# DeltaNet with mixture-of-depths: the query-key products masked on other engines, one join product moved to another PSUM bank, and a re-tuned plan

## The chip, the cores and the metric

The kernel runs on one core of a Trainium2 chip. A core has a matrix engine (TensorE, "PE" in the profile, with its weight loads as "PEld"), VectorE (DVE), ScalarE (ACT), GpSimd (POOL) and SyncE (SP), which issues most DMAs. Each engine works through its own queue in order and waits at semaphores for the others. The metric is the device time of one execution, in microseconds (us).

## The reference

Inputs are q, k, v of shape (batch 4, heads 8, 768 tokens, head size 48) and beta. For each of the 32 batch-head pairs a 48x48 state is carried over the tokens; its output is then the input x of a mixture-of-depths block.

```python
k_n = k / (norm(k) + 1e-6)
for t in range(768):
    y[t] = q[t] @ state                              # read before the update
    state += beta[t] * outer(k_n[t], v[t] - k_n[t] @ state)

x = y as (4, 768, 384)
scores = x @ w_gate
for b in range(4):
    top = the 128 tokens of the highest score
    out = x;  out[top] += sigmoid(scores[top]) * (relu(x[top] @ w1) @ w2)
```

## The kernel before

The tokens are cut into chunks of 64. Batches go in two groups of two, so there are 24 units (`NU`): chunks 0 to 11 of group 0, then chunks 0 to 11 of group 1. Within a chunk the recurrence is a triangular system. Its 64x64 matrices are cut into 32x32 diagonal blocks, and those of four units (128 of them, one on each partition) are inverted together: that is an *elimination* (`eliminate(e)`, six of them, e = 0 to 5).

- `prep(i)`: transposes k and q through PSUM (L437), copies them out on ACT (L442), multiplies k by k (to `gs`, spilled to DRAM by SP, L503, and read back as `a`) and q by k (to `p`). The q-k product lies in two PSUM banks of the ring `inv` (three banks). In the kernel before, DVE takes it out and masks it with the strict upper triangle in one instruction for each bank (`out_p`, L507): 48 in all.
- `eliminate(e)`: all on DVE but two steps. The norms (L567 to L582), the scaling of `a` (L592), a copy of `a` into PSUM by ACT (`lift`, L596), the unit diagonal (L599), 30 pairs of a multiply (L608) and a subtract (L615), each of which needs the one before, the mask (`final`, L621) and two transposes (`turn_out` L624, `turn_back` L628). POOL makes the table `mb` (L585) and copies half-blocks of `tt` (`lows`, L716).
- `join(e, m)`: for each unit of the four, PE makes `z` (L688, L690), ACT copies it (`ez`, L694), PE makes two products (L701, L703), ACT copies them into `tt` (`ej`, L710).
- `recur(i)`: the chain from unit to unit: PE `mm_r` into `prec` (L750), DVE adds it to v (L757), PE `mm_w` (L763), two ACT copies (L768), PE `mm_s` (L774), two ACT copies (L781), and then the next unit's `mm_r`. Beside it `mm_q` (L790) and `mm_p` (L801) build the output in the bank `py`, and ACT takes it out (L807). `mm_p` needs the masked `p`. POOL scales v (L742) and multiplies the output by the gate weights (L824).
- `ranking(g)` and `depths(b)`: comparisons of the scores (POOL L909 and L913, at the very end DVE), their sums on PE (L937), the choice (DVE L979), gather, two layers (L1035, L1049), scatter. Those of group 0 are mixed in with the recurrence of group 1; those of group 1 are the tail.

The order on every engine is written by `Plan`: a list scheduler that runs when the program is built. Each step has a length, dependences, a priority (`prio`; smaller goes first) and tokens that it takes and gives back (`ring`, such as the three `inv` banks). Whatever the planner's times are, what runs on the chip is the resulting order on each queue. Where it foresees a gap on PE, it puts in filler matmuls (`filler`, L348) that have no use but to keep PE active.

Of the kernel before, what the change touches and what calls it, by code (L numbers as in the profile page):

```python
# [185 lines left out]
def kernel(  # L186
# [24 lines left out]
    GP = GB * HP  # L211
    GI = GP // 2
# [18 lines left out]
    plan = Plan()  # L231
    rings = {}
# [36 lines left out]
    py = psum.tile([P, 512], FP32, name="py")  # L269
# [5 lines left out]
    rings["late"] = [ap[:, m] for m in range(2)]  # L275
    plan.ring("late", 2)
    first_g = rings["tt"][1]

    def got(*key):
        name, m = plan.live[key]  # L280
        return rings[name][m]

    def maker(eng, own=0.0, lat=0.15):
        def add(dur, emit, deps=(), prio=0.0, take=(), give=(), lat=lat, hard=False, ins=0,
                dmas=0, moves=0.56, room=None):
            op = plan.add(eng, dur, emit, deps, prio,
                          [(t[0] if isinstance(t, tuple) else t, t) for t in take],
                          give, lat)
            op.own, op.hard, op.ins, op.dmas = own, hard, ins, dmas
            op.moves, op.room = moves, room  # L290
            return op
        return add

    pe, act, dve, pool, sp = [maker(*e) for e in (
        ("PE", 0.0, 0.22), ("ACT", 0.0, 0.12), ("DVE", 0.12, 0.2), ("POOL",), ("SP",))]
# [135 lines left out]
    N = {}  # L431
# [14 lines left out]
    def prep(i):  # L446
# [10 lines left out]
        def bank(key):  # L457
            return got(*key)[:, :GI * C].rearrange("p (r t) -> p r t", t=C)
# [46 lines left out]
        def out_p(rt):  # L505
            def emit():
                nc.vector.tensor_tensor(  # L507
                    out=got("p", i).rearrange("p (r b) t -> p r b t", b=2)[:, :, rt],
                    in0=bank(kw[rt]), op=ALU.mult,
                    in1=up[:, None, :].to_broadcast([P, GI, C]))  # L510
            return emit

        n["lk"] = sp(0.65 if first else 1.25,
# [6 lines left out]
        for nm in "kq":  # L520
            emit, put = turn(i, nm)
            v, h = (u - 2, hard) if nm == "k" else (10 * i - 20, {})
            n["t" + nm] = pe(0.46, emit, [n["l" + nm]], v, ins=2 * GI,
                             take=[("inv", i, nm), (nm + "t", i)],
                             give=[("q", i)] if nm == "q" else [], **h)
            n["e" + nm] = act(0.6, put, [n["t" + nm]], v, give=[("inv", i, nm)], **h)
# [4 lines left out]
        else:  # L531
# [8 lines left out]
                    ins=16 * GI, lat=0.8)  # L540
        n["ep"] = [dve(0.43, out_p(rt), [n["w"]], v, give=[kw[rt]]) for rt in range(2)]

    def eliminate(e):
# [98 lines left out]
        N["nrm", e] = s["nt"] = dve(0.2, turn_n, [s["sc"]], u + 2)  # L642
        s["mb"] = pool(1.3, table, [s["sc"]], u, take=[("mb", e)])
        last = dve(1.2, scale, [s["sc"]], u, **hard)
# [8 lines left out]
        N["steps", e] = last  # L653
        last = dve(1.15, final, [last, s["mb"]], u, **hard)
        N["final", e] = last
# [13 lines left out]
    def join(e, m):  # L669
# [5 lines left out]
        s, n = N["e", e], N[i]  # L675
        key = {w: ("inv", i, w) for w in ("z", "ja", "jb")}

        def view(w):
            return got(*key[w])[:, :GI * HC].rearrange("p (n t) -> p n t", t=HC)

# [47 lines left out]
    def recur(i):  # L728
# [98 lines left out]
        def total():  # L827
# [4 lines left out]
                     take=[("v", i)], dmas=2, room=1.0)  # L832
        x = r["vh"] = pool(1.1, vh, [n["lv"], N["e", e]["nt"]], u - 12, lat=0.3)
        if c > 0:
# [15 lines left out]
        if c > 0:  # L850
            r["q"] = pe(0.7, mm_q, qdep + [*o["es"], n["eq"], o.get("xo")], u + 3, ins=8 * GI)
            pdep = [r["q"]]
        r["p"] = pe(0.7, mm_p, [*r["w"], *n["ep"], o.get("xo")] + qdep + pdep, u + 3, ins=8 * GI,
                    give=[("kt", i), ("qt", i), ("p", i)])
        plan.add("PE", 0.0, lambda: None, [r["p"], r.get("s")], 10 * i, give=[("k", i)])
        r["xo"] = act(0.48, out_x, [r["p"]], u + 4, take=[("x", j)] if i % 2 == 0 else [],
                      lat=0.12 if i == NU - 1 else 2.0)
        late = i >= NU - 2
        if late:
            N["score", i] = dve(0.65, score, [r["xo"], N["wg"]], u + 12, give=[("x", j)])  # L860
        else:
            pr0 = pool(1.1, score, [r["xo"], N["wg"]], u + 12, take=[("prod", i)],
                       give=[("x", j)], lat=1.0)
            N["score", i] = act(0.52, total, [pr0], u + 14, give=[("prod", i)])
# [9 lines left out]
    def ranking(g):  # L874
# [4 lines left out]
        def stage(j0, j1, prev):  # L879
# [75 lines left out]
            for j in range(j0, j1):  # L955
                d.append((dve if soon else pool)(
                             0.37 + 0.26 * (j > 0) + 0.067 * j if soon else
                             0.5 + 0.08 * (j + 1), above(j), [a1] + (d or tests)[-1:], u + 1,
                             take=[km] if j == j0 else [],
                             give=[("rep", g)] if last else [], **hd))  # L960
# [178 lines left out]
```

## Time and profile before

| | |
|---|---|
| median of three runs | 331.19 us (330.13 to 333.48) |
| the profiled execution | 330.42 us |
| its span in the trace | 328.6 us |
| PE busy | 294.1 us, of it 51.3 us fillers |
| DVE busy | 210.3 us |
| ACT busy | 177.1 us |
| POOL busy | 126.5 us |

Busy times of a stretch are sums over an engine's instructions. Matmuls are pipelined, so a PE that shows 90% is not at its peak. A wait counts only if the engine that waits is the one that others wait for in that stretch. The first 57 us are loading and elimination 0, 57 to 283 us the recurrence of the 24 units, the rest the tail.

### The profile page before, as it was taken

What the parts mean: (1) busy time and instruction counts of PE and PEld (TensorE: products, weight loads), DVE (VectorE), ACT (ScalarE), POOL (GpSimd) and SP (SyncE); (2) the same over time, 40 slices, a digit from 0 to 9 for tenths busy, and PEclk for the clock granted to TensorE, in tenths of its full rate; (3) what the DMA queues carried; (4) which work ended last, traced back from release to release, by engine and by line L of the source; (5) the groups of instructions that cost most, each with busy time, mean ns of one, the idle gap of its engine ahead of it and who ended that gap; (6) DMA issues with size and microseconds to landing.
All of it is one profiled execution on the core that took longest, in us unless ns stands there. A gap on an engine that the chain in (4) does not pass through costs nothing.

```text
span 328.6 us, 15204 instructions
## 1 busy us (share of the span) xinstructions
PE 294.1 (90%) x6583; PEld 229.5 (70%) x6603; DVE 210.3 (64%) x580; ACT 177.1 (54%) x490; POOL 126.5 (39%) x199
## 2 busy tenths in 40 slices
PE   7879999899979999689959989799988999989993
PEld 2766444688857887468847867588877898667781
DVE  6037999798866889979878799759991102342000
ACT  1446000877667768677576864765876566211120
POOL 8105103721482338426293463820827243122011
PEclk9959999999997999999985999879999799999999
DMA  7967896246876486835764229526301021102000
GB/s 129 139 113 162 189 276 200 40 118 154 165 145 144 117 161 108 216 88 93 159 126 92 58 103 182 102 50 128 81 6 48 4 51 27 26 26 64 8 26 24
DMA packets 116083, 34.05 MB, mean 104 GB/s; under 512 B 108432, under 2 KB 112656, under 8 KB 116016
## 3 DMA queue, kind: packets, MB, share of 16 engines
q1 hardware_dynamic: 113392, 31.11, 45.0%
q0 software_dynamic: 512, 1.57, 1.5%
q8 instruction: 52, 0.85, 1.1%
q10 hardware_dynamic: 2112, 0.39, 0.8%
q14 instruction: 15, 0.12, 0.1%
HBM read 22.32 MB, written 10.75 MB: 101 GB/s over the span
## 4 chain that ended last, share of the span: by engine, by line
PE 66%; issue 10%; ACT 8%; DVE 6%; POOL 5%; DMA 2%; SPq 1%; POOLq 0%; ACTq 0%; DVEq 0%
PE inv L348 13%; PE prec L763 6%; PE inv L437 6%; PE inv L491 5%; PE psta L774 5%; PE py L801 4%; PE ap L1035 4%; PE py L790 4%; PE prec L750 4%; PE ap L1049 3%; POOL mk L909 3%; ACT wbd L768 2%; PE inv L701 2%; PE inv L1035 2%; PE inv L1049 2%
## 5 line engine op out<-in xcount | busy, mean ns | idle before, releaser
L615 DVE TENSOR_TENSOR ap<-ap,tmp 128x30 f32<-128x30 f32 (+9 forms) x180 | 60.5, 336 | 5.0
L608 DVE TENSOR_TENSOR tmp<-a,ap 128x30 f32<-128x30 f32 (+9 forms) x180 | 58.5, 325 | 5.0
L348 PE MATMUL inv<-warm 128*128 128x512 bf16 x187 | 51.3, 401 | 5.3 <-DVE warm L362 2.1
L824 POOL TENSOR_TENSOR prod<-x,wg 128x384 f32<-128x384 f32 x22 | 23.9, 1088 | 37.4 <-ACT x L807 37.2
L742 POOL TENSOR_TENSOR v<-v,nnT 128x384 f32<-128x384 f32 x24 | 19.7, 828 | 47.0 <-DMA v<-in_v_dram 46.9
L348 PEld LDWEIGHTS <-warm 128*128 128x128 bf16 x207 | 19.8, 102 | 23.0 <-issue 3.3
L909 POOL TENSOR_SCALAR mk<-rep 128x64 bf16<-128x64 f32 (+11 forms) x22 | 27.5, 1250 | 19.0 <-ACT rep L901 16.2
L768 ACT COPY wbd<-prec 64x384 f32<-64x384 f32 x48 | 22.7, 473 | 16.2 <-PE prec L763 11.6
L757 DVE TENSOR_TENSOR v<-v,prec 128x384 f32<-128x384 f32 x22 | 12.2, 553 | 28.7 <-PE prec L750 15.3
L716 POOL COPY tt<-tt 32x256 f32<-32x256 f32 x48 | 19.5, 406 | 25.4 <-DVE tt L624 21.1
L710 ACT COPY tt<-inv 32x128 f32<-32x128 f32 x96 | 24.6, 256 | 7.5 <-PE inv L703 5.4
L763 PEld LDWEIGHTS prec<-v,tt 64*64 64x64 f32 x768 | 25.2, 138 | 4.8 <-issue 2.4
L763 PE MATMUL prec<-v,tt 64*64 64x48 f32 x768 | 28.1, 223 | 0.3
L781 ACT COPY s<-psta 64x384 f32<-64x384 f32 x44 | 20.8, 473 | 9.9 <-PE psta L774 9.5
L774 PE MATMUL psta<-wbd,k 128*48 128x96 f32 x352 | 21.5, 268 | 3.8 <-ACT wbd L768 2.9
L774 PEld LDWEIGHTS psta<-wbd,k 128*48 128x48 f32 x352 | 16.5, 133 | 9.4 <-ACT wbd L768 6.2
L801 PE MATMUL py<-wbd,p 128*64 128x96 f32 x384 | 21.8, 260 | 0.0
L585 POOL TENSOR_SCALAR_AFFINE_SELECT mb<-bh 128x1024 f32<-128x1024 f32 x6 | 11.6, 1941 | 24.9 <-DVE bh L579 24.9
L442 ACT COPY kt<-inv 128x512 f32<-128x512 f32 x24 | 14.1, 591 | 13.1 <-PE inv L437 12.9
L790 PE MATMUL py<-s,qt 128*64 128x96 f32 x352 | 20.1, 260 | 0.0
L507 DVE TENSOR_TENSOR p<-inv,up 128x256 f32<-128x256 f32 x48 | 19.5, 415 | 0.4 <-PE inv L491 0.2
L801 PEld LDWEIGHTS py<-wbd,p 128*64 128x64 f32 x384 | 18.7, 147 | 1.2 <-ACT spr L890 0.5
(151 smaller groups left out, 609.4 us busy)
## 6 DMA issues: line engine op xcount, KB each, us to landing
gd<-gs SPq DMA_DIRECT2D x20, 256.0 KB, 2.9
v<-in_v_dram SPq DMA_DIRECT2D x48, 96.0 KB, 3.2
q<-in_q_dram SPq DMA_DIRECT2D x48, 96.0 KB, 3.1
k<-in_k_dram SPq DMA_DIRECT2D x44, 96.0 KB, 3.5
out_dram<-x SPq DMA_DIRECT2D x20, 192.0 KB, 3.2
a<-gd SPq DMA_DIRECT2D x20, 128.0 KB, 3.4
w_sb<-in_moe_w_dram SPq DMA_DIRECT2D x3, 512.0 KB, 4.9
w_sb<-in_moe_w_dram SPq DMA_DIRECT2D x4, 384.0 KB, 4.6
```

Source lines behind the costliest of these rows:

```text
L348: nc.tensor.matmul(rings[name][k], lhsT=warm[:, :P], rhs=warm, start=True, stop=True)
L608: nc.vector.tensor_tensor(out=view(), op=ALU.mult, in0=got("a", e)[:, j + 1:, j:j + 1].to_broadcast([P, w, j]), in1=blocks[:, j:j + 1, :j] ...
L615: nc.vector.tensor_tensor(out=a[:, j + 1:, :j], in0=a[:, j + 1:, :j], in1=view(), op=ALU.subtract)
L710: nc.scalar.copy(to[lo[par], :, int(w == "jb"), HC:], view(w)[lo[par]])
L763: nc.tensor.matmul(pw[half[par], a], lhsT=tt[half[par], ch * GP + a], rhs=x[half[par], a], start=True, stop=True)
L768: nc.scalar.copy(wb[half[par], :, par], pw[half[par]])
L774: nc.tensor.matmul(psta[ds[a % 2], a // 2], lhsT=t[:, a, :D], rhs=wb[:, a].rearrange("p h d -> p (h d)"), start=(c == 0 and a < 2), stop=True,
L781: nc.scalar.copy(s_new[half[rt], :, :, rt], psta[half[rt]].rearrange("p a (x d) -> p a x d", d=D))
L790: nc.tensor.matmul(pyv[half[bb], h4, :, par], lhsT=qt[:, bb * 2 + h4, half[par]], rhs=s_old[:, bb * 2 + h4, par], start=(h4 == 0 and par = ...
L801: nc.tensor.matmul(pyv[half[bb], h4, rt], lhsT=t[:, a], rhs=wb[:, a], start=(c == 0 and h4 == 0 and rt == 0), stop=True, skip_group_check= ...
L824: nc.gpsimd.tensor_tensor(out=got("prod", i), in0=got("x", i // 2)[:, i % 2], in1=wg, op=ALU.mult)
L909: nc.gpsimd.tensor_scalar(out=mk[:, :(j + 1) * C].rearrange("p (j c) -> p j c", c=C), in0=rep[:, :j + 1, :C], scalar1=rep[:, j, C:], scala ...
```

## The change

Four things. (1) The q-k product is copied out of PSUM by ACT, unmasked, and POOL then masks all of it in place in SBUF, with one instruction for each unit. (2) `z` is written to columns 384 to 511 of the bank `py`, which the output (columns 0 to 383) leaves free, and no longer to an `inv` bank; `py` becomes a ring of one, taken by `mm_q` (or `mm_p` where there is none) and given back by the copy L807, and taken by `z` and given back by `ez`. (3) Some lengths in the plan are set to other values. (4) A table `SHIFT` adds an offset to the priority of 50 kinds of steps.

```diff
+SHIFT = {
+    "ACT:<lambda>": -28.4, "ACT:ej": 7.8, "ACT:ez": -7.3, "ACT:gate0": -2.7, "ACT:lift": -12.0,
...
+    "turn_k": -26.5,
+}
+def kind(eng, emit):
...
+    rings["py"] = [py]
+    plan.ring("py", 1)
+    assert DM + GI * HC == 512
...
-            op = plan.add(eng, dur, emit, deps, prio,
+            op = plan.add(eng, dur, emit, deps, prio + SHIFT.get(kind(eng, emit), 0.0),
...
         def out_p(rt):
             def emit():
-                nc.vector.tensor_tensor(
-                    out=got("p", i).rearrange("p (r b) t -> p r b t", b=2)[:, :, rt],
-                    in0=bank(kw[rt]), op=ALU.mult,
-                    in1=up[:, None, :].to_broadcast([P, GI, C]))
+                nc.scalar.copy(got("p", i).rearrange("p (r b) t -> p r b t", b=2)[:, :, rt],
+                               bank(kw[rt]))
             return emit
+
+        def mask():
+            t = got("p", i)
+            nc.gpsimd.tensor_tensor(out=t, in0=t, op=ALU.mult,
+                                    in1=up[:, None, :].to_broadcast([P, GP, C]))
...
-            n["t" + nm] = pe(0.46, emit, [n["l" + nm]], v, ins=2 * GI,
+            n["t" + nm] = pe(0.9, emit, [n["l" + nm]], v, ins=2 * GI,
...
-        n["ep"] = [dve(0.43, out_p(rt), [n["w"]], v, give=[kw[rt]]) for rt in range(2)]
+        n["ep"] = [act(0.38, out_p(rt), [n["w"]], v, give=[kw[rt]]) for rt in range(2)]
+        n["ep"] = [pool(1.3, mask, n["ep"], v)]
...
-        s["mb"] = pool(1.3, table, [s["sc"]], u, take=[("mb", e)])
+        s["mb"] = pool(1.8, table, [s["sc"]], u, take=[("mb", e)])
...
-        key = {w: ("inv", i, w) for w in ("z", "ja", "jb")}
+        key = {w: ("inv", i, w) for w in ("ja", "jb")}
+        key["z"] = ("py", i, "z")
...
-            r["q"] = pe(0.7, mm_q, qdep + [*o["es"], n["eq"], o.get("xo")], u + 3, ins=8 * GI)
+            r["q"] = pe(0.7, mm_q, qdep + [*o["es"], n["eq"]], u + 3, ins=8 * GI, take=[("py", i)])
...
-                             0.5 + 0.08 * (j + 1), above(j), [a1] + (d or tests)[-1:], u + 1,
+                             0.6 + 0.16 * (j + 1), above(j), [a1] + (d or tests)[-1:], u + 1,
```

What the change does to the order is seen at three places. Line numbers of the changed kernel are about 30 higher: L638 and L645 are the multiply and subtract of the elimination, L789 the addition to v, L539 the mask on POOL.

The first is DVE in elimination 1, around the addition of unit 1 (`v1`), before:

```order
L615 TENSOR_TENSOR ap_141<-ap_141,tmp_170 128x23x8
L608 TENSOR_TENSOR tmp_170<-a1_112,ap_141 128x198
L757 TENSOR_TENSOR v1_79<-v1_79,prec_139 128x384
L615 TENSOR_TENSOR ap_141<-ap_141,tmp_170 128x22x9
L608 TENSOR_TENSOR tmp_170<-a1_112,ap_141 128x210
L507 TENSOR_TENSOR p1_102<-inv0_136,up_153 128x4x64
L615 TENSOR_TENSOR ap_141<-ap_141,tmp_170 128x21x10
L507 TENSOR_TENSOR p1_102<-inv2_138,up_153 128x4x64
L608 TENSOR_TENSOR tmp_170<-a1_112,ap_141 128x220
```

and of the change:

```order
L638 TENSOR_TENSOR tmp_170<-a1_112,ap_141 128x198
L645 TENSOR_TENSOR ap_141<-ap_141,tmp_170 128x22x9
L638 TENSOR_TENSOR tmp_170<-a1_112,ap_141 128x210
L645 TENSOR_TENSOR ap_141<-ap_141,tmp_170 128x21x10
L638 TENSOR_TENSOR tmp_170<-a1_112,ap_141 128x220
L645 TENSOR_TENSOR ap_141<-ap_141,tmp_170 128x20x11
L789 TENSOR_TENSOR v1_79<-v1_79,prec_139 128x384
L638 TENSOR_TENSOR tmp_170<-a1_112,ap_141 128x228
L645 TENSOR_TENSOR ap_141<-ap_141,tmp_170 128x19x12
```

The masking is gone from between the steps, and the addition stands five steps later.

The second is DVE where elimination 2 is prepared (`a0`): the scaling, the transpose of the norms, and the memset of the diagonal, which waits for ACT's `lift`. Before:

```order
L579 TENSOR_TENSOR bh0_168<-bh0_168,bt_143 128x32
L592 TENSOR_TENSOR a0_111<-a0_111,bh0_168 128x1024
L582 STREAM_TRANSPOSE nnT2_167<-nrm_164 128x32
L599 MEMSET ap_141 128x32
L608 TENSOR_TENSOR tmp_170<-a0_111,ap_141 128x30
L615 TENSOR_TENSOR ap_141<-ap_141,tmp_170 128x30
```

and of the change, whose memset L629 stands two rows behind the last one shown:

```order
L622 TENSOR_TENSOR a0_111<-a0_111,bh0_168 128x1024
L638 TENSOR_TENSOR tmp_170<-a1_112,ap_141 128x84
L789 TENSOR_TENSOR v3_81<-v3_81,prec_139 128x384
L645 TENSOR_TENSOR ap_141<-ap_141,tmp_170 128x3x28
L612 STREAM_TRANSPOSE nnT2_167<-nrm_164 128x32
L638 TENSOR_TENSOR tmp_170<-a1_112,ap_141 128x58
L645 TENSOR_TENSOR ap_141<-ap_141,tmp_170 128x2x29
L638 TENSOR_TENSOR tmp_170<-a1_112,ap_141 128x30
L645 TENSOR_TENSOR ap_141<-ap_141,tmp_170 128x30
L651 TENSOR_TENSOR a1_112<-ap_141,mb1_120 128x1024
L654 STREAM_TRANSPOSE tt1_124<-a1_112 128x32x32
L658 STREAM_TRANSPOSE mb1_120<-a1_112 128x32x32
```

The scaling of block 2 now stands ahead of the end of block 1, so that the two transposes lie between the mask of block 1, behind which `lift` may start, and the memset.

The third is POOL at the join of elimination 3: `lows` (L716, now L748) and the comparisons of the ranking (L909, now L941). Before:

```order
L585 AFFINE_SELECT mb_119<-bh_168 128x1024
L824 TENSOR_TENSOR prod_129<-x_126,wg 128x384
L909 TENSOR_SCALAR mk_130<-rep_127 128x576
L913 TENSOR_TENSOR mk_130<-mk_130,trib 128x64
L909 TENSOR_SCALAR mk_130<-rep_127 128x640
L913 TENSOR_TENSOR mk_130<-mk_130,trib 128x64
L716 COPY tt_124<-tt_124 32x8x32 x8
L824 TENSOR_TENSOR prod_129<-x_126,wg 128x384
```

and of the change:

```order
L941 TENSOR_SCALAR mk_130<-rep_127 128x512
L945 TENSOR_TENSOR mk_130<-mk_130,trib 128x64
L774 TENSOR_TENSOR v_81<-v_81,nnT_165 128x384
L856 TENSOR_TENSOR prod_129<-x_125,wg 128x384
L748 COPY tt_124<-tt_124 32x8x32 x4
L539 TENSOR_TENSOR p_104<-p_104,up 128x512
L748 COPY tt_124<-tt_124 32x8x32 x4
L615 AFFINE_SELECT mb_119<-bh_168 128x1024
L856 TENSOR_TENSOR prod_129<-x_126,wg 128x384
```

The two long comparisons are no longer ahead of `lows`, and a mask stands between its halves.

On PE the order has 107 fillers where it had 207; the q-k products of units 1 to 3, the k-k products of units 8 to 11 and the transposes that these need now stand ahead of the first `z`; the transposes of beta (L304) stand behind all products of the first four units, where they stood in the middle; and two `z` never stand next to each other. Ahead of the end of elimination 5, DVE now has the addition of unit 18 as its last, where it had that of unit 19.

## Rows read from the trace of the kernel before

**Rows 1.** The page's first part: busy us (share) x instructions of each engine.

```profile
PE 294.1 (90%) x6583; PEld 229.5 (70%) x6603; DVE 210.3 (64%) x580; ACT 177.1 (54%) x490; POOL 126.5 (39%) x199
```

**Rows 2.** Busy time by stretch: PE, PEld, DVE, ACT, POOL; granted clock; DMA.

```profile
57.00:247.00 190.00, 170.75 (x4725) 141.85 (x4738) 159.11 (x436) 134.38 (x377) 88.46 (x115) 0.95 0.55 115
247.00:283.00 36.00, 33.66 (x769) 28.67 (x767) 5.01 (x14) 23.18 (x70) 15.63 (x22) 0.95 0.13 32
```

**Rows 3.** Timeline of DVE, eliminations 0 and 1: start, length, line [idle before].

```profile
28.18 0.09 DVE L599 MEMSET ap<- 128x32 f32 x1 [1.06 <-ACT ap L596]
...
50.40 1.23 DVE L621 TENSOR_TENSOR a<-ap,mb 128x1024 f32<-128x1024 f32 x1
...
59.65 0.09 DVE L599 MEMSET ap<- 128x32 f32 x1 [1.01 <-ACT ap L596]
```

**Rows 4.** Timeline of DVE at the end of elimination 5.

```profile
241.56 1.23 DVE L621 TENSOR_TENSOR a<-ap,mb 128x1024 f32<-128x1024 f32 x1
```

**Rows 5.** Timeline of DVE: the same steps without masking (elimination 0) and with (1).

```profile
34.14 0.37 DVE L608 TENSOR_TENSOR tmp<-a,ap 128x210 f32<-128x210 f32 x1
34.55 0.39 DVE L615 TENSOR_TENSOR ap<-ap,tmp 128x210 f32<-128x210 f32 x1
...
66.66 0.38 DVE L608 TENSOR_TENSOR tmp<-a,ap 128x210 f32<-128x210 f32 x1
66.95 0.42 DVE L507 TENSOR_TENSOR p<-inv,up 128x256 f32<-128x256 f32 x1
67.28 0.38 DVE L615 TENSOR_TENSOR ap<-ap,tmp 128x210 f32<-128x210 f32 x1
```

**Rows 6.** The page's groups: the masking on DVE.

```profile
L507 DVE TENSOR_TENSOR p<-inv,up 128x256 f32<-128x256 f32 x48 | 19.5, 415 | 0.4 <-PE inv L491 0.2
```

**Rows 7.** Waits: who waited for whom, us in total, times, longest.

```profile
DVE v L757 <- PE prec L750: 15.3, 10, 4.8
...
DVE ap L599 <- ACT ap L596: 7.9, 5, 2.7
```

**Rows 8.** Timelines of PE and DVE at the start.

```profile
15.04 0.87 PE L304 MATMUL inv<-ident,both 32*64 32x16 f32 x24 [1.38 <-issue]
...
21.05 1.95 DVE L551 STREAM_TRANSPOSE a<-tt 128x1024 f32<-128x1024 f32 x1 [4.06 <-ACT tt L481]
```

**Rows 9.** Groups nearest to what is added: busy us, mean ns, idle before.

```profile
L824 POOL TENSOR_TENSOR prod<-x,wg 128x384 f32<-128x384 f32 x22 | 23.9, 1088 | 37.4 <-ACT x L807 37.2
...
L498 ACT COPY gs<-inv 128x256 f32<-128x256 f32 x40 | 13.1, 374 | 6.2 <-PE inv L491 6.1
...
L807 ACT COPY x<-py 128x384 f32<-128x384 f32 x24 | 11.5, 481 | 4.9 <-PE py L801 4.5
...
L694 ACT COPY zt<-inv 128x128 f32<-128x128 f32 x24 | 6.4, 267 | 15.4 <-PE inv L690 15.0
```

**Rows 10.** Timelines of DVE and POOL: the scaling and the table side by side.

```profile
127.41 1.23 DVE L592 TENSOR_TENSOR a<-a,bh 128x1024 f32<-128x1024 f32 x1
127.45 2.31 POOL L585 TENSOR_SCALAR_AFFINE_SELECT mb<-bh 128x1024 f32<-128x1024 f32 x1 [1.45 <-DVE bh L579]
...
161.97 1.27 POOL L585 TENSOR_SCALAR_AFFINE_SELECT mb<-bh 128x1024 f32<-128x1024 f32 x1 [6.41 <-DVE bh L579]
```

**Rows 11.** Timeline of DVE: the additions of units 19, 21 and 23.

```profile
238.89 0.55 DVE L757 TENSOR_TENSOR v<-v,prec 128x384 f32<-128x384 f32 x1 [0.19 <-PE prec L750]
...
260.61 0.55 DVE L757 TENSOR_TENSOR v<-v,prec 128x384 f32<-128x384 f32 x1 [4.77 <-PE prec L750]
...
273.41 0.56 DVE L757 TENSOR_TENSOR v<-v,prec 128x384 f32<-128x384 f32 x1 [5.64 <-ACT x L807]
```

**Rows 12.** The chain that ended last, in the tail: start, length, what.

```profile
301.40 5.39 PE inv L1035 x48
```

**Rows 13.** Timeline of POOL at the join of elimination 3.

```profile
164.19 1.72 POOL L909 TENSOR_SCALAR mk<-rep 128x576 bf16<-128x576 f32 x1
...
168.99 3.49 POOL L716 COPY tt<-tt 32x256 f32<-32x256 f32 x8
```

More of the change, by code (lines that the diff above doesn't have):

```diff
@@ L21 @@
 LAND = 2.6
+SHIFT = {
+    "ACT:<lambda>": -28.4, "ACT:ej": 7.8, "ACT:ez": -7.3, "ACT:gate0": -2.7, "ACT:lift": -12.0,
+    "ACT:out_beta": -6.9, "ACT:out_g": -2.4, "ACT:out_h": 14.6, "ACT:out_p": 8.8,
+    "ACT:out_s": -9.5, "ACT:out_w": 0.2, "ACT:out_x": 1.4, "ACT:out_xt": -2.2, "ACT:root": -19.2,
+    "ACT:spot": 4.2, "ACT:total": -0.2, "DVE:<lambda>": 41.4, "DVE:above": -5.6,
+    "DVE:choose": -10.5, "DVE:final": 4.3, "DVE:gate1": 13.0, "DVE:out_idx": 6.6,
+    "DVE:out_o": -9.1, "DVE:out_p": -29.2, "DVE:rescore": 1.1, "DVE:scale": -42.0,
+    "DVE:scales": -12.7, "DVE:score": 6.9, "DVE:turn_n": -0.7, "DVE:unit": 0.2, "PE:jj": -21.4,
+    "PE:mm_g0": -38.6, "PE:mm_idx": 4.3, "PE:mm_q": -0.3, "PE:mm_r": -6.9, "PE:mm_s": -11.3,
+    "PE:mm_w": 8.0, "PE:sums": 1.8, "PE:turn_x": -41.8, "POOL:gather": -10.5, "POOL:lows": 7.2,
+    "POOL:mask": 4.7, "POOL:score": 16.7, "POOL:table": 4.3, "POOL:zeros": -9.9, "SP:put": -35.1,
+    "SP:spill": -41.8, "load_k": -14.8, "load_q": 9.4, "load_v": -11.7, "products_kt": -18.3,
+    "turn_k": -26.5,
+}
+def kind(eng, emit):
+    path = emit.__qualname__.split(".")
+    name = path[-1] if path[-1] != "emit" else path[-3]
+    held = dict(zip(emit.__code__.co_freevars, emit.__closure__ or ()))
+    if name in ("turn", "out", "load", "products") and "nm" in held:
+        return name + "_" + held["nm"].cell_contents
+    return eng + ":" + name
 class Op:
@@ L653, in eliminate @@
         N["steps", e] = last
-        last = dve(1.15, final, [last, s["mb"]], u, **hard)
+        last = dve(1.23, final, [last, s["mb"]], u, **hard)
         N["final", e] = last
@@ L675, in join @@
         s, n = N["e", e], N[i]
-        key = {w: ("inv", i, w) for w in ("z", "ja", "jb")}
+        key = {w: ("inv", i, w) for w in ("ja", "jb")}
+        key["z"] = ("py", i, "z")
         def view(w):
-            return got(*key[w])[:, :GI * HC].rearrange("p (n t) -> p n t", t=HC)
+            x = got(*key[w])
+            return (x[:, DM:] if w == "z" else x[:, :GI * HC]).rearrange("p (n t) -> p n t", t=HC)
         def z():
@@ L832, in recur @@
                      take=[("v", i)], dmas=2, room=1.0)
-        x = r["vh"] = pool(1.1, vh, [n["lv"], N["e", e]["nt"]], u - 12, lat=0.3)
+        x = r["vh"] = pool(0.85, vh, [n["lv"], N["e", e]["nt"]], u - 12, lat=0.3)
         if c > 0:
@@ L850, in recur @@
         if c > 0:
-            r["q"] = pe(0.7, mm_q, qdep + [*o["es"], n["eq"], o.get("xo")], u + 3, ins=8 * GI)
+            r["q"] = pe(0.7, mm_q, qdep + [*o["es"], n["eq"]], u + 3, ins=8 * GI, take=[("py", i)])
             pdep = [r["q"]]
-        r["p"] = pe(0.7, mm_p, [*r["w"], *n["ep"], o.get("xo")] + qdep + pdep, u + 3, ins=8 * GI,
-                    give=[("kt", i), ("qt", i), ("p", i)])
+        r["p"] = pe(0.7, mm_p, [*r["w"], *n["ep"]] + qdep + pdep, u + 3, ins=8 * GI,
+                    take=[] if pdep else [("py", i)], give=[("kt", i), ("qt", i), ("p", i)])
         plan.add("PE", 0.0, lambda: None, [r["p"], r.get("s")], 10 * i, give=[("k", i)])
-        r["xo"] = act(0.48, out_x, [r["p"]], u + 4, take=[("x", j)] if i % 2 == 0 else [],
+        r["xo"] = act(0.48, out_x, [r["p"]], u + 4, give=[("py", i)], take=[("x", j)] if i % 2 == 0 else [],
                       lat=0.12 if i == NU - 1 else 2.0)
@@ L861, in recur @@
         else:
-            pr0 = pool(1.1, score, [r["xo"], N["wg"]], u + 12, take=[("prod", i)],
+            pr0 = pool(1.05, score, [r["xo"], N["wg"]], u + 12, take=[("prod", i)],
                        give=[("x", j)], lat=1.0)
```

## The prediction

> **What bounds the kernel now.** I read the busy table first, then the stretches, then DVE's own timeline, then who waits for whom. The busy table [rows 1] makes PE the suspect, at 90% of the span. The stretches correct that: between 57 and 247 us, in which the five later eliminations run, PE is busy for 170.8 of 190 us, a figure that includes waits inside its pipeline, and DVE for 159.1 [rows 2]. Behind 247 us DVE has 5 us of work in 36. So something that only DVE does ends near 247. Its timeline shows what: `final` (L621), which closes an elimination, starts at 50.40 for the first [rows 3], and at 241.56 for the sixth [rows 4], so 191.2 us for five blocks, 38.2 each. With nothing between its steps, elimination 0 went from the memset at 28.18 to `final` at 50.40, 22.2 us, and from there to the memset of the next it was 9.3 us (50.40 to 59.65). A block thus costs DVE 31.5 us at the least. The other 6.7 us of a block are maskings, additions to v, and waits: for `mm_r` 15.3 us in all, of which 4.8 fall behind the last block, so 10.5 us, and for ACT's `lift` 7.9 us [rows 7]. The recurrence itself needs less: the additions of units 21 and 23 are 12.8 us apart [rows 11], 6.4 us a unit and 25.6 for the four units of a block. Between 57 and 247 us the kernel runs at DVE's pace, and the recurrence has some 10 us a block to spare.
>
> **What the change takes from that pace.**
>
> *Maskings off DVE.* 48 instructions of 415 ns leave [rows 6], 19.5 us. That is not what the pace gains. Step L608 of 210 elements started 0.41 us before its L615 when alone (34.14, 34.55) and 0.62 us with a masking between them (66.66, 67.28) [rows 5]. The step after a masking waits 0.33 us for it, but 0.12 of that is a gap that the two dependent steps leave anyway. So a masking costs 0.21 us. 44 of the 48 stand ahead of the end of elimination 5: 44 x 0.21 = 9.2 us. The bounds are 8 us (some stand where DVE waits anyhow) and the full 44 x 0.415 = 18.3; I take 9.2, since most stand between two steps.
>
> *`lift` out of the way.* DVE waited 7.9 us for it, at least 1.0 each time [rows 3, 7]. In the new order the scaling of block 2 stands ahead of the end of block 1, so that the two transposes cover `lift`; in block 5 the choice of the tokens covers it, and in block 4 an addition covers half. Left are 1.06 for block 0, 1.0 each for blocks 1 and 3, 0.5 for block 4: 3.6. Gain 4.3 us; between 0, if other work delays ACT as it did before, and 6.8.
>
> *The start.* DVE's first transpose waited 4.06 us for the products of the first four units, and PE's transposes of beta stood between them, with 1.38 us in which PE waited for nothing but its own instructions [rows 8]. They now come behind the products. The time in which instructions arrive is not saved by a new order, so the bounds are 0 and 2.3 us (1.38 + 0.87); I take 1.0.
>
> *Additions and the end of block 5.* DVE now has the addition of unit 18 as its last before that end, where it had 19. That costs nothing: before, unit 21 was added 21.7 us after unit 19 [rows 11], because the join of block 5 had to come first. Now unit 19 comes some 5 us behind the start of block 5's `final` (itself and the two transposes: in the blocks shown, 9.3 us lie between `final` and the next memset, and they are the larger half), and four units follow at 6.4 us plus about 1 us for the join: 5 + 4 x 6.4 + 1 = 31.6 us from that start to the addition of unit 23. Before it was 273.41 - 241.56 = 31.9.
>
> *The tail.* Nine of the 24 first-layer products of batch 0 now stand behind the last `mm_w`. 24 products of that shape, 48 matmuls in the trace, take 5.39 us [rows 12], so nine are 2.0 us. They lie in the wait for the last ranking; without that cover they would cost those 2.0.
>
> **What it adds.**
>
> *ACT.* 48 copies of this shape at 374 ns [rows 9], 18.0 us, 16.5 of them before the end of block 5. ACT was busy for 134.4 of 190 us; with 151 in some 176 it is at 86%, no bound, but every copy on the recurrence (L768, L781) can find one of the new ones in front. If each of 20 units lost 0.374 us, that is 7.5; the recurrence has 10 us a block to spare, so I take 2, between 0 and 7.5.
>
> *POOL.* 24 masks of 512 elements. The nearest row, the same operation on 384, took 1.09 us [rows 9]; a mask is between that and 4/3 of it, 1.45. That is 35 us at most on an engine that had 88.5 us in 190, so it is hidden unless the order is bad (a rival below). One part is not: when DVE's scaling ran from 127.41, the table on POOL that started with it took 2.31 us, against 1.27 us when it ran alone [rows 10]. The two hold each other up. A mask on POOL may thus hold up the scaling in each of five blocks, by 1.45 us at most, 7.3 in all; POOL will be masking for a sixth of the time, so I take 1. The Trainium skill (SBUF — State Buffer, section Who interferes with whom) says that a DVE instruction with two SBUF inputs and a GpSimd instruction that reads SBUF exclude each other for their whole length, whichever came first; by the full rule with a mask always first the sum below would end at 326, and the trace agrees on the exclusion. The steps of the elimination read one operand from PSUM, and the same page leaves such instructions out of it.
>
> *`z` in `py`.* Two `z` can no longer be issued together; the second waits for the copy of the first, 267 ns [rows 9]. 20 joins behind the first block could each put that on PE: 5.3 us. PE has other work in the order between two `z`, and a block has time to spare: 1 us, between 0 and 5.3.
>
> *Plan lengths.* They change only the order; costed with it. The 100 fillers that leave stood in gaps, and nothing waits for them. If PE's granted clock fell without them from 0.95 [rows 2] to 0.90, its 170.8 us would be 180 of the same 190, which works for the first rival.
>
> **Sum.** From the profiled execution, 330.42 us (0.2% under the median of the three runs): - 9.2 - 4.3 - 1.0 + 2 + 1 + 1 = 319.9. I forecast **320 us**, chance 0.50.
>
> **Rivals.**
>
> *The recurrence takes over the pace* (0.21). If PE and ACT, and not DVE, space the units, then each addition waits on DVE for what the maskings no longer fill, and 10.5 us of waiting for `mm_r` become 20 or more. For it: PE at 90%, ACT going to 86%, and units spaced by 9.6 us within the blocks (38.2 / 4), where the end shows 6.4. Against it: the waits for `mm_r` were only 2.1 us a block, and k and q work has moved ahead of the first `z`. The maskings' gain and `lift`'s are lost: 330.4 - 1 = 329.5, or up to 332 with the added work.
>
> *The waits go too* (0.13). The same lighter stretch on PE may bring `mm_r` ahead of every addition. Then 10.5 us more are gained: 309.5. For it: the additions stand later in the order, as the one of unit 1 does. Against it: a faster DVE reaches them sooner.
>
> *A mask stuck behind POOL's long work stops PE* (0.16), slower. `mm_p` needs the mask, the output's copy needs `mm_p`, and now `z` needs that copy, as both use `py`; PE stands in order behind them. At the join of elimination 3 POOL worked without a gap from 164.19 to 172.48, 8.3 us of comparisons and half-block copies [rows 13]. A mask that meets such a run adds 8.3 + 1.45 + 2 x 0.374 us, and four `z` that each wait for an output copy and a `z` copy add 4 x (0.48 + 0.27) [rows 9]: 13.5 us a block. The first 10 us are spare, so five blocks cost 5 x 3.5 = 18 us: 338. It turns the result to slower from 12 to 13 us a block. For it: the order puts masks right beside `lows` and comparisons. Against it: the two longest comparisons no longer stand ahead of `lows` of elimination 3.
>
> **Numbers.** The range of 308 to 333 holds the forecast with its bounds, the rival at 309.5 and the one at 330 to 332; what it leaves out is most of the slower rival and a sliver below. About 1% is what a measurement can tell from no change, so faster is below 327.9 and slower above 334.5, from the median of 331.19. Faster: 0.49 of the forecast, 0.13, and a quarter of the first rival (0.05): 0.67. Within 1%: 0.01, most of the first rival (0.13), and 0.02 of the slower one: 0.16. Slower: 0.03 and 0.14: 0.17.
>
> **What would show it.** Right: the `final` of two eliminations 35 to 36 us apart; steps L638 and L645 at 0.41 us wherever no addition stands between; waits for `lift` of 1.0 us or none; ACT busy for about 195 us, POOL for 152 to 161. The first rival shows as waits of L789 for `mm_r` well above 10.5 us with blocks still near 38; the slower one as PE idle until an output or `z` copy, with POOL's L539 as the cause; the exclusion as a scaling L622 longer than 1.25 us. I am wrong if the blocks come down to 35 and the end does not follow, since then the stretch behind elimination 5 has grown.

## The result, and the profile after

The changed kernel takes **318.03 us**, median of four runs (315.91 to 320.75), against 331.08 (330.13 to 333.48) in the same comparison: a ratio of 0.957, 95% interval 0.950 to 0.964. Ratios and intervals here leave out runs in a slower state that an execution of any kernel can fall into; medians and ranges are over all runs. The forecast was 320. The number was right; its reason was not. DVE did not set the pace. What made the kernel faster is the order of the queues, and the traces show two places where most of it was gained.

The profiled execution took 318.92 us, its span 317.2. The page's busy table, which answers to [rows 1]:

```profile
PE 277.5 (87%) x6503; PEld 223.4 (70%) x6503; DVE 201.1 (63%) x532; ACT 189.7 (60%) x538; POOL 156.8 (49%) x223
```

The stretches of [rows 2], with the same columns:

```profile
57.00:247.00 190.00, 166.82 (x4754) 141.86 (x4754) 151.42 (x392) 143.94 (x419) 114.27 (x141) 0.93 0.56 118
247.00:283.00 36.00, 34.12 (x607) 28.84 (x604) 8.64 (x27) 18.77 (x54) 15.55 (x16) 1.00 0.11 30
```

DVE's timeline, the first and the sixth `final` (`final` is now L651), which answer to [rows 3, 4]:

```profile
49.72 1.23 DVE L651 TENSOR_TENSOR a<-ap,mb 128x1024 f32<-128x1024 f32 x1
...
228.96 1.23 DVE L651 TENSOR_TENSOR a<-ap,mb 128x1024 f32<-128x1024 f32 x1
```

The five blocks take 179.2 us, 35.8 each on average, against 191.2 and 38.2: the forecast's very figure. But they are uneven, from 28.4 to 40.3 us, as they were before (33.8 to 41.5): only as a mean does a distance of 35 to 36 us hold. The waits of [rows 7] and [rows 8], and the groups of the mask and of the fillers:

```profile
DVE v L789 <- PE prec L782: 19.7, 6, 7.4
...
DVE a L581 <- ACT tt L507: 13.4, 1, 13.4
...
DVE ap L629 <- ACT ap L626: 4.4, 4, 1.8
```

```profile
L539 POOL TENSOR_TENSOR p<-p,up 128x512 f32<-128x512 f32 x24 | 31.2, 1304 | 29.6 <-ACT p L533 29.4
L374 PE MATMUL inv<-warm 128*128 128x512 bf16 x107 | 31.2, 415 | 3.0 <-DVE warm L388 2.1
```

So far most looks as forecast: the mask takes 1.30 us, `lift` is waited for 4.4 us instead of 7.9 (the longest wait 1.8). The 13.4 us before DVE's first transpose are no new loss: the transposes of beta, which broke up that wait before, now stand behind it. Two things do not fit. The page's chain that ended last gave DVE little of the path before, a row that the prediction did not use; first the kernel before, then the changed one:

```profile
PE 66%; issue 10%; ACT 8%; DVE 6%; POOL 5%; DMA 2%; SPq 1%; POOLq 0%; ACTq 0%; DVEq 0%
```

```profile
PE 45%; DVE 24%; issue 10%; ACT 9%; DMA 7%; SPq 2%; POOL 1%; POOLq 0%; DVEq 0%; ACTq 0%
```

With 6% of the chain, DVE is an unlikely engine to set the pace. This is a hint and no more: the changed kernel has DVE at 24%, and the runs below show that its load is not the bound there either. And the gain does not come evenly block by block. These are the starts of the additions to v, which carry the state from unit to unit, from DVE's timeline (us):

| unit | 1 | 4 | 11 | 13 | 14 | 16 | 19 | 20 | 21 | 23 |
|---|---|---|---|---|---|---|---|---|---|---|
| before | 65.79 | 93.08 | 162.19 | 182.50 | 196.45 | 220.34 | 238.89 | 246.64 | 260.61 | 273.41 |
| after | 68.50 | 95.14 | 161.41 | 179.16 | 185.83 | 210.34 | 233.98 | 240.56 | 248.50 | 260.56 |
| difference | +2.7 | +2.1 | -0.8 | -3.3 | -10.6 | -10.0 | -4.9 | -6.1 | -12.1 | -12.9 |

Of the 12.9 us, 7.3 come in one step, from unit 13 to 14 (13.95 us before, 6.67 after), and 6.0 in another, from 20 to 21 (13.97 and 7.94). What lies between them and ahead of them nearly cancels. From the last addition to the end of the span 1.4 us are given back (55.2 before, 56.6 after). These are single executions: other runs of the new order, below, have the addition of unit 1 anywhere from 66.3 to 69.9 us.

### The profile page after: what moved, and what is told of

Same layout as the page of the kernel before. It is cut to its first block, busy times and chain, and to the rows that moved or that the text cites. A ratio compares the mean times of both kernels' runs of the same rounds, so it can differ in the third digit from the quotient of the medians.

```text
span 317.2 us, 15007 instructions
## 1 busy us (share of the span) xinstructions
PE 277.5 (87%) x6503; PEld 223.4 (70%) x6503; DVE 201.1 (63%) x532; ACT 189.7 (60%) x538; POOL 156.8 (49%) x223
## 3 DMA queue, kind: packets, MB, share of 16 engines
q0 software_dynamic: 512, 1.57, 1.6%
## 4 chain that ended last, share of the span: by engine, by line
PE 45%; DVE 24%; issue 10%; ACT 9%; DMA 7%; SPq 2%; POOL 1%; POOLq 0%; DVEq 0%; ACTq 0%
DVE ap L645 6%; DVE tmp L638 6%; PE prec L795 5%; PE psta L806 4%; PE inv L463 4%; PE ap L1067 4%; PE ap L1081 4%; PE inv L374 3%; PE inv L517 3%; PE py L833 3%; DMA a<-gd 3%; PE prec L782 2%; DVE mb L658 2%; PE py L822 2%; DMA k<-in_k_dram 2%
## 5 line engine op out<-in xcount | busy, mean ns | idle before, releaser
L645 DVE TENSOR_TENSOR ap<-ap,tmp 128x30 f32<-128x30 f32 (+9 forms) x180 | 60.8, 338 | 5.7
L638 DVE TENSOR_TENSOR tmp<-a,ap 128x30 f32<-128x30 f32 (+9 forms) x180 | 58.9, 327 | 5.8
L539 POOL TENSOR_TENSOR p<-p,up 128x512 f32<-128x512 f32 x24 | 31.2, 1304 | 29.6 <-ACT p L533 29.4
L374 PE MATMUL inv<-warm 128*128 128x512 bf16 x107 | 31.2, 415 | 3.0 <-DVE warm L388 2.1
L789 DVE TENSOR_TENSOR v<-v,prec 128x384 f32<-128x384 f32 x22 | 12.1, 551 | 34.0 <-PE prec L782 19.7
L795 PE MATMUL prec<-v,tt 64*64 64x48 f32 x768 | 28.8, 227 | 5.2 <-DVE v L789 4.6
L941 POOL TENSOR_SCALAR mk<-rep 128x64 bf16<-128x64 f32 (+11 forms) x22 | 27.5, 1249 | 11.4 <-ACT rep L933 8.5
L795 PEld LDWEIGHTS prec<-v,tt 64*64 64x64 f32 x768 | 26.0, 142 | 8.8 <-DVE v L789 4.0
L800 ACT COPY wbd<-prec 64x384 f32<-64x384 f32 x48 | 22.7, 473 | 12.5 <-PE prec L795 11.3
L856 POOL TENSOR_TENSOR prod<-x,wg 128x384 f32<-128x384 f32 x22 | 24.0, 1092 | 10.9 <-ACT x L839 10.7
L748 POOL COPY tt<-tt 32x256 f32<-32x256 f32 x48 | 21.1, 440 | 11.2 <-DVE tt L654 7.9
L806 PE MATMUL psta<-wbd,k 128*48 128x96 f32 x352 | 20.7, 264 | 3.0 <-ACT wbd L800 2.9
L463 PE MATMUL inv<-ident,k 128*128 128x128 f32 x96 | 16.0, 310 | 6.9 <-DMA k<-in_k_dram 4.7
L1091 POOL DMA_INDIRECT out_dram<-oe,idx x4 | 4.0, 1008 | 34.5 <-DVE oe L1086 19.4
L615 POOL TENSOR_SCALAR_AFFINE_SELECT mb<-bh 128x1024 f32<-128x1024 f32 x6 | 9.5, 1582 | 22.3 <-DVE bh L609 22.1
L782 PE MATMUL prec<-s,kt 128*64 128x96 f32 x352 | 20.0, 259 | 0.0
```

Source lines behind the costliest of these rows:

```text
L374: nc.tensor.matmul(rings[name][k], lhsT=warm[:, :P], rhs=warm, start=True, stop=True)
L463: nc.tensor.transpose(ps[:, r * P:(r + 1) * P], x[:, 2 * r:2 * r + 2].rearrange("p b d -> p (b d)"), ident)
L539: nc.gpsimd.tensor_tensor(out=t, in0=t, op=ALU.mult, in1=up[:, None, :].to_broadcast([P, GP, C]))
L638: nc.vector.tensor_tensor(out=view(), op=ALU.mult, in0=got("a", e)[:, j + 1:, j:j + 1].to_broadcast([P, w, j]), in1=blocks[:, j:j + 1, :j] ...
L645: nc.vector.tensor_tensor(out=a[:, j + 1:, :j], in0=a[:, j + 1:, :j], in1=view(), op=ALU.subtract)
L782: nc.tensor.matmul(pr[half[par], a * 2 * D:(a + 1) * 2 * D], lhsT=kt[:, a, half[par]], rhs=s_old[:, a, par].rearrange("p r d -> p (r d)"), ...
```

## The experiments

Medians, with the ratio to the kernel before on the same chip, whose median was 330.7 to 331.0 each time.

**The new instructions in the old order.** Every queue as in the kernel before; ACT's copies stand where DVE's maskings stood, a mask on POOL behind every second one.

```diff
-                nc.vector.tensor_tensor(out=got("p", i)..., in0=bank(kw[rt]), op=ALU.mult, in1=up...)
+                nc.scalar.copy(got("p", i)..., bank(kw[rt]))
+                if rt == 1:
+                    nc.gpsimd.tensor_tensor(out=t, in0=t, op=ALU.mult, in1=up...)
```

> The order of every engine as before; only the masking is taken off DVE: where DVE masked, ACT copies, and POOL masks behind the second copy. If DVE's steps set the pace, each of the 44 maskings that leave gives 0.21 us back: 331 - 9 = 322, between 319 and 325 us. If the recurrence sets it and the maskings only filled time in which DVE waited, the additions wait for mm_r by as much more and the time stays at 329 to 332 us. If the order of before leaves the new copies and masks at bad places on ACT and POOL, it is slower than 333.

343.81 us, ratio 1.046 (1.035 to 1.057). Then the same without the mask, so that the products stay unmasked:

> As the kernel with the old order and the masking moved (343.8 us), but POOL's mask is left out, so that the q-k products stay unmasked; the ACT copies stay. If the 13 us that it lost come from masks that stand ahead of POOL's comparisons, for which ACT's counts (L927 before) wait, they go: 322 to 331 us, and waits of ACT for POOL fall from 11.1 us to the 2.6 us of before. If the ACT copies in front of the recurrence's own copies cost them: 339 to 344 us.

332.63 us, ratio 1.006 (1.001 to 1.011). So 48 instructions less on DVE with 48 more on ACT, in an order that stays, gained nothing: the time is 1.7 us longer, by the interval 0 to 4, and as much above the range expected if the masks were to blame. The masks cost 11 us. Who waited, in the first of the two:

```profile
POOL p L511 <- ACT p L507: 43.6, 19, 7.3
...
ACT mute L929 <- POOL mk L915: 11.1, 12, 1.7
```

and the second of these in the kernel before:

```profile
ACT mute L927 <- POOL mk L913: 2.6, 3, 1.3
```

POOL stands before its mask until ACT has copied; the ranking's comparisons stand behind it, and ACT's counts (`mute`) wait for those, with the copies of the recurrence behind them. Without the masks that wait is back at 2.6 us. That this wait is how the masks cost their 11 us is read from the traces, not tested by itself. This is the slower rival's kind of stall, though it went through ACT's counts and not through `py`.

**The new order with the masking back on DVE**, at the place of the copies, and no mask on POOL.

```diff
-                nc.scalar.copy(got("p", i)..., bank(kw[rt]))
+                nc.vector.tensor_tensor(out=got("p", i)..., in0=bank(kw[rt]), op=ALU.mult, in1=up...)
...
         def mask():
+            pass
```

> The order of every engine as in the changed kernel; only the two ACT copies and the POOL mask of each unit are replaced by the two maskings on DVE, at the place of the copies. If DVE's steps set the pace: 318 + 9 = 327, between 324 and 330 us. If the new order is what pays and maskings fill waits: 318 to 321 us.

324.84 us, ratio 0.986 (0.979 to 0.993). The order alone, with DVE as loaded as ever, gives 6 of the 13 us (by the interval 2 to 7); the unit from 13 to 14 takes 6.85 us here too. The addition of unit 17 still lies within 0.7 us of the changed kernel's, that of unit 20 is 5.1 us behind. DVE's timeline there, then PE's:

```profile
232.24 1.96 DVE L654 STREAM_TRANSPOSE tt<-a 128x1024 f32<-128x1024 f32 x1
234.06 0.40 DVE L533 TENSOR_TENSOR p<-inv,up 128x256 f32<-128x256 f32 x1
234.38 2.02 DVE L658 STREAM_TRANSPOSE mb<-a 128x1024 f32<-128x1024 f32 x1
236.33 0.38 DVE L533 TENSOR_TENSOR p<-inv,up 128x256 f32<-128x256 f32 x1
```

```profile
234.51 0.26 PE L969 MATMUL inv<-warm,mk 64*64 64x1 bf16 x6 [0.98 <-DVE p L533]
236.76 0.38 PE L374 MATMUL inv<-warm 128*128 128x512 bf16 x1 [1.45 <-DVE p L533]
```

PE waits for banks of `inv` that two maskings hold, and these stand behind transposes of 2 us. The second of these rows is a filler: it needs a bank too and comes as late. The stall costs more than its length. Two stretches of PE, with the columns of [rows 2], then `mm_w` of unit 19 here and in the changed kernel:

```profile
233.00:237.00 4.00, 1.57 (x16) 1.23 (x16) 4.00 (x5) 2.01 (x7) 2.44 (x7) 1.00 0.00 0
237.00:241.00 4.00, 3.95 (x86) 3.63 (x89) 0.24 (x2) 0.28 (x2) 3.71 (x7) 0.57 0.02 4
```

```profile
239.09 1.84 PE L795 MATMUL prec<-v,tt 64*64 64x48 f32 x32
...
234.61 1.14 PE L795 MATMUL prec<-v,tt 64*64 64x48 f32 x32
```

After 4 us in which PE was busy for 1.57, its granted clock was 0.57, near the lower of its two levels, for the next 4. `mm_w` started 2.45 us behind its addition, where the changed kernel has 0.63, and took 0.7 us longer: together 2.5 us, and unit 20 falls 2.4 us further behind than unit 19 had. So what moving the masking is worth in this order lies mostly here: a bank no longer waits in DVE's queue. It is not spread over the blocks, as 0.21 us for each masking would be.

The time itself, 324.84, lies in the range that was set for DVE's pace, and so do those of the offsets and lengths alone and of the masking alone further below. By their times these three would speak for the prediction's account; what speaks against it is where the time is lost here, and the runs with half of the steps.

**The mask left out of the new order** (products unmasked, all else as changed; `mask()` emits nothing).

> The changed kernel with POOL's mask left out (the products stay unmasked) and everything else in the same order. If the masks cost 1 us in the new order, as the prediction's sum has it: 317, between 315 and 319 us. If they hold up POOL's other work or DVE's scaling (which took up to 2.30 us beside them): 310 to 314 us, with scalings of 1.25 us.

320.09 us, ratio 0.965 (0.955 to 0.975), no faster than with the mask and above both forecasts. In the new order the masks cost nothing that these runs can tell.

**`z` back in `inv`, planned anew** (the diff's lines on `key["z"]` and `py` undone).

> The changed kernel, planned again with z in the three inv banks and py outside the plan as before. If z in py costs what the prediction took, 1 us: about 317. If the inv banks that it frees are what lets the key and query work move ahead: 321 to 327 us.

320.27 us, ratio 0.970 (0.962 to 0.978). The intervals overlap the changed kernel's: `z` in `py` is worth 2 us or nothing, between the two forecasts.

**No offsets** (`prio + SHIFT.get(...)` becomes `prio`).

> The changed kernel with all 50 offsets of priority at zero; the moved masking, z in the bank py and the new lengths stay. If the relief of DVE is the larger part, as in the prediction's sum (9.2 of 13.5 us), about 322, between 319 and 326 us. If the offsets make the gain: 328 us or more.

330.54 us, ratio 0.999 (0.994 to 1.004): the whole gain is gone, with masking and `z` where the change put them.

**Offsets and lengths alone** (masking on DVE, `z` in `inv`), and **the masking alone** (the kernel before's lengths and priorities; copies and mask are in its plan, so the planner orders all queues anew).

> The offsets and the new lengths alone: the masking stays on DVE and z in the ring inv. If the relief of DVE is the larger part, the order gives only what lift and the start do, about 5 us: 326, between 323 and 330 us. If the order is what pays: 318 to 322 us. The offsets were set for another structure, so that a time above 331 speaks against neither.

> The kernel before with the masking moved to ACT and POOL in the plan, so that the planner orders it; lengths, priorities and z as before. If the planner of before can use the relief of DVE: 322 to 326 us. If the relief needs the offsets (without them the changed kernel took 330.5): 328 to 334 us. If the lengths of before put masks at the same bad places as in the old order: 338 or more.

323.10 us, ratio 0.983 (0.974 to 0.991), and 323.37 us, ratio 0.970 (0.960 to 0.980; its four runs spread from 318 to 327). Each alone gives about half or more of the gain, with wide intervals; they do not add, since each is another order. The masking alone needed no offsets for its gain, while the new lengths and `z` in `py` without offsets (330.54) have none: no single item of the change carries the whole of it.

**Half of the elimination left out.** Every second pair of steps emits nothing in eliminations 1 to 5, which are then incomplete; the queues' order is untouched. First in the changed kernel, then in the kernel before.

```diff
             def mul():
+                if e and j % 2 == 0:
+                    return
...
             def sub():
+                if e and j % 2 == 0:
+                    return
```

> The changed kernel, its order untouched, with every second pair of steps (L638, L645) left out of eliminations 1 to 5, so that the blocks are not fully inverted; elimination 0 keeps all of them. That takes some 11 us of DVE out of each of the five blocks. DVE's pace (the prediction's view): a block falls from 35.8 us to what the recurrence of four units needs, 25.6 us or little more, and the time to 318 - 5 x 9 = 273 us, at most 285. The recurrence spaces the units: DVE only waits longer for mm_r, blocks stay within 1.5 us of 35.8, and the time at 311 to 318 us. A time half-way (290 to 305) would say that both take turns.

> The same halving of the steps in eliminations 1 to 5 (which are then left incomplete) in the kernel before, in its own order. DVE's pace: blocks of 38.2 us fall by some 10 us each, the time from 331 to about 281 us, at most 295. The recurrence spaces the units: the time stays at 323 to 331 us and the waits of DVE for mm_r grow from 15 us to 60 or more.

320.78 us, ratio 0.969 (0.964 to 0.974), and 331.09 us, ratio 1.004 (1.000 to 1.009). DVE's busy time falls by 49 us in the one and by 46 in the other, and the time does not fall in either. The busy table of the changed kernel with half of the steps, and its wait for `mm_r`:

```profile
PE 276.8 (87%) x6487; PEld 225.6 (71%) x6503; DVE 152.1 (48%) x382; ACT 189.8 (59%) x538; POOL 157.3 (49%) x223
...
DVE v L793 <- PE prec L786: 53.1, 12, 8.0
```

Of the 49 us that DVE saved, 33 went into longer waits for `mm_r` (19.7 us with all steps), the rest into other waits. In the kernel before, those for `mm_r` grew less than expected, from 15.3 us:

```profile
DVE v L761 <- PE prec L754: 26.9, 9, 7.5
...
DVE p L507 <- PE inv L491: 10.9, 12, 1.8
```

The second line was 0.2 us with all steps, and the rest went into waits for ACT, POOL and the ranking's sums. In the changed kernel the `final` of two eliminations stay 35.9 us apart on average although a block has some 10 us less to do: they stand in DVE's queue behind additions, and keep the additions' pace. The time, 320.78, is some 3 us above the range expected for a recurrence that spaces the units, and 36 above the one for DVE's pace. This settles it for both kernels: the load of DVE's elimination is not the bound.

**Twice the copies on ACT** (each copy of a q-k product made twice; ACT is busy for 16 us more) and **no fillers on PE** (`range(n)` becomes `range(0)` in `filler`).

> The changed kernel with each of ACT's copies of the q-k product made twice (48 more copies of 374 ns, 18 us of ACT); order and result as they are. DVE's pace: ACT, at 60% of the span, has room, 318 to 320 us. The recurrence spaces the units, with ACT's copies on its way: one or two of the added copies in front of each of 20 units, 0.37 to 0.75 us each, 325 to 333 us.

> The changed kernel without its 107 filler matmuls on PE (31 us of busy time that computes nothing), all else in its order. The prediction took fillers as free and said that nothing waits for them. DVE's pace: even at a lower granted clock the waits for mm_r stay small, 317 to 323 us. The recurrence spaces the units, so PE's clock counts: if the granted clock falls from 0.94 to 0.85 or less, a tenth on PE's part of a block, 330 us or more; if the clock holds, 316 to 318 us.

321.26 us, ratio 0.965 (0.956 to 0.973), and 322.59 us (317.63 to 324.33), ratio 0.976 (0.971 to 0.982). The second set of copies cost about 3 us, with intervals that overlap the changed kernel's: between the two forecasts. Without fillers the kernel was not faster. But the granted clock fell with them, to 0.864 to 0.900 over the four runs (0.936 to 0.951 with fillers), and the run at 0.900 was the fastest; so this run does not tell apart what fillers hold up and what they give back in clock, and its time, in the range for DVE's pace, decides nothing.

The two steps in which the gain lay, over the profiled executions in order of the last addition:

| run | median | unit 13 to 14 | 20 to 21 | last addition |
|---|---|---|---|---|
| old order, masks on POOL | 343.8 | 13.3 | 14.6 | 285.9 |
| old order, copies only | 332.6 | 13.3 | 12.8 | 273.9 |
| before | 331.1 | 14.0 | 14.0 | 273.4 |
| before, half of the steps | 331.1 | 13.5 | 14.8 | 273.1 |
| no offsets | 330.5 | 11.3 | 11.8 | 268.4 |
| offsets and lengths alone | 323.1 | 11.1 | 10.7 | 268.1 |
| masking alone | 323.4 | 15.4 | 11.0 | 266.8 |
| new order, masking on DVE | 324.8 | 6.8 | 8.0 | 265.8 |
| after, copies twice | 321.3 | 6.7 | 8.0 | 263.0 |
| after, half of the steps | 320.8 | 6.5 | 7.9 | 262.3 |
| after, `z` in `inv` | 320.3 | 9.1 | 6.4 | 261.9 |
| after, no mask | 320.1 | 6.7 | 7.9 | 261.0 |
| after | 318.0 | 6.7 | 7.9 | 260.6 |
| after, no fillers | 322.6 (this execution 317.6) | 6.7 | 8.1 | 259.3 |

Runs with one order share their two steps, nearly, whatever the load of DVE or POOL: 13.3 to 14.0 and 12.8 to 14.8 us in the old order, 6.5 to 6.9 and 7.9 to 8.1 in the new. But they are no law for other orders: the masking alone has the longest first step of all, and its last addition still comes 6.6 us earlier than before. No run moved only what stands at these two places, so that they make the gain is read from the traces. (Without offsets the time is longer than the last addition tells: its tail takes 59.2 us, where the others take 53 to 57.)

## What the two steps are

Unit 14 in the kernel before, DVE's timeline up to its addition, then PE's `mm_r`:

```profile
192.71 0.17 DVE L975 TENSOR_TENSOR rank<-count 128x12 f32<-128x12 f32 x1
192.91 0.17 DVE L976 TENSOR_TENSOR rank<-rank,csum 128x12 f32<-128x12 f32 x1
193.00 0.33 DVE L615 TENSOR_TENSOR ap<-ap,tmp 128x168 f32<-128x168 f32 x1
193.24 1.75 DVE L979 TENSOR_TENSOR sel<-iota_r,rank 128x1536 bf16<-128x1536 f32 x1
194.91 0.30 DVE L608 TENSOR_TENSOR tmp<-a,ap 128x150 f32<-128x150 f32 x1
195.36 0.42 DVE L507 TENSOR_TENSOR p<-inv,up 128x256 f32<-128x256 f32 x1
195.70 0.31 DVE L615 TENSOR_TENSOR ap<-ap,tmp 128x150 f32<-128x150 f32 x1
195.92 0.41 DVE L507 TENSOR_TENSOR p<-inv,up 128x256 f32<-128x256 f32 x1
196.25 0.28 DVE L608 TENSOR_TENSOR tmp<-a,ap 128x130 f32<-128x130 f32 x1
196.45 0.55 DVE L757 TENSOR_TENSOR v<-v,prec 128x384 f32<-128x384 f32 x1
```

```profile
190.96 0.88 PE L750 MATMUL prec<-s,kt 128*64 128x96 f32 x16
```

`mm_r` was done at 191.84 and its addition started 4.6 us later, without any idle time, so that no list of waits shows it. Ahead of it in the queue stood the choice of group 0's tokens, which needs the ranking's last sums. With half of the steps left out, in the same order, DVE idles there and the addition comes at nearly the same time:

```profile
192.09 0.17 DVE L947 TENSOR_TENSOR csum<-csum,inv 128x12 f32<-128x12 f32 x1 [2.49 <-PE inv L941]
...
195.98 0.55 DVE L761 TENSOR_TENSOR v<-v,prec 128x384 f32<-128x384 f32 x1
```

In the changed kernel the choice stands elsewhere. PE, then DVE:

```profile
184.14 0.88 PE L782 MATMUL prec<-s,kt 128*64 128x96 f32 x16
```

```profile
185.56 0.36 DVE L645 TENSOR_TENSOR ap<-ap,tmp 128x184 f32<-128x184 f32 x1
185.83 0.54 DVE L789 TENSOR_TENSOR v<-v,prec 128x384 f32<-128x384 f32 x1
```

0.8 us from `mm_r` to the addition, so 3.8 of the 7.3 us. The other 3.5 lie between the addition of unit 13 and `mm_r` of 14 (8.46 us before, 4.98 after): on ACT the two copies of unit 13's `mm_w` started 1.79 us apart (184.73 and 186.52), with copies of k-k products and of k between them; now they stand together, from 181.21. That is 1.5 us; another 0.9 lie on ACT ahead of the copies of `mm_s`, and 1.1 on PE, where k-k products and transposes of k stood ahead of `mm_s` and `mm_r`.

Unit 21 is the first to need elimination 5. Before, `final` came at 241.56 [rows 4], behind the addition of unit 19, and the join followed the addition of unit 20. ACT's copies of `z` ran from 248.0 to 254.8 us, all behind it. Now `final` comes at 228.96, ahead of unit 19, and those copies run from 234.8 to 244.8, mostly beside units 19 and 20. The forecast costed this at nothing, and from `final` to the last addition it is: 31.6 us, as forecast. But `final` itself came early because the additions ahead of it did. So the second step mostly gives back what units 17 to 20 lost by standing beside the join: the lead was 10.6 us at unit 14, 4.9 at unit 19 and 12.9 at the end.

## Why the prediction was right, and where not

That the number came out within 2 us was luck: 13.5 of the 14.5 us that the sum takes off rest on a pace of DVE that the runs do not bear out.

- **What bounds the kernel** failed, and with it the sum's main term. That `final` after `final` lies 38.2 us apart was read as DVE's pace. It is the additions' pace: DVE works in order, and `final` stands behind them. Half of the steps taken away moved neither (320.78 us and 331.09). The 31.5 us "at the least" also held waits, and blocks from 33.8 to 41.5 us long were a sign against one steady pace. The chain that ended last (DVE 6%) spoke for the first rival.
- **Maskings, 9.2 us at 0.21 each.** Without a masking the steps do lie 0.41 us apart. As relief of DVE that is worth nothing: no gain in the old order, none from half of the steps in either order. In the new order moving the masking is worth 7 us (324.84 to 318.03). Of the 5.2 us between the last additions of the two profiled executions, 4.4 lie at units 18 to 20, where banks of `inv` were given back late. The size was near by luck.
- **`lift`, 4.3 us.** The waits fell by 3.5 us; since ten us less work of DVE in a block changed nothing, these cannot have counted as such.
- **The start, 1.0 us.** The first transpose starts 0.7 us sooner (21.05 to 20.33), but the first addition 2.7 us later (0.5 to 4.1 in the other runs of this order).
- **ACT +2, POOL +1, `z` +1**: not contradicted in size. 48 more copies cost about 3 us on top, the masks nothing in this order, `z` nothing measurable. The mask's 1.30 us lies within its bounds; ACT was busy for 189.7 us, not the 195 that was named as a sign.
- **The tail at 0**: it grew by 1.4 us.
- **Left out of the sum**: the order itself. It was costed through what DVE waits for; it is worth 6 us alone and decides over the rest, 343.8 with the same instructions in the old order and 330.5 without offsets.
- **The first rival** was right that DVE does not space the units, and had the price wrong: some 332 is what the relief of DVE gives in a fixed order (332.63 measured, without masks). That PE and ACT space them instead is not shown. Its sign in the trace was to be longer waits for `mm_r` "with blocks still near 38"; the blocks shrank with the additions. Blocks 35.8 us apart fit either theory, so that test told nothing apart.

Left open: what sets the 8 to 10 us of a unit in the middle, where the last three take 6. PE is busy for 87% of the span. The load of DVE's elimination is not it; twice the copies on ACT cost 3 us, so ACT's load is not it alone; PE's fillers and clock were not told apart. The kernel before without its 207 fillers was not run.

## What to carry to other kernels

The distance between two instructions of one engine is that engine's pace only if nothing of another stands between them in its queue; take half of its work away in the same order before a saving on it is priced. Its share of the chain that ended last is a hint only: DVE had 6% before and 24% after, and halving its steps helped in neither. In a tuned kernel of in-order queues, follow the values that go from one unit to the next, and for each compare when the last input was there with when the step began: a queue that is late though never idle shows in no list of waits. A new instruction on an idle engine costs what stands behind it, and the same 24 masks cost 11 us in one order and nothing measurable in another.

## What was unexpected of the hardware

The scaling in elimination 2 took 2.30 us, and it did so without any mask as well (from 86.76 in that run). DVE's row, then POOL's, of the changed kernel:

```profile
85.87 2.30 DVE L622 TENSOR_TENSOR a<-a,bh 128x1024 f32<-128x1024 f32 x1
```

```profile
85.84 1.26 POOL L615 TENSOR_SCALAR_AFFINE_SELECT mb<-bh 128x1024 f32<-128x1024 f32 x1 [7.08 <-DVE bh L609]
87.08 1.95 POOL L856 TENSOR_TENSOR prod<-x,wg 128x384 f32<-128x384 f32 x1
```

The table started 0.03 us ahead and ran its 1.26 us; the scaling, 1.2 us by itself, ended 1.07 us behind the table's end, and the next work on POOL took 1.95 us instead of 1.09. In [rows 10] the scaling was first and the table stretched. In these rows whichever came first held the other up. The Trainium skill (SBUF — State Buffer, section Who interferes with whom) says the same of two such instructions.
